# A fused attention and MLP kernel: batch 0 laid out in 96 partitions, a new placing of the second block, a bank read moved by one unit, and the last stores on three queues

## The chip, the cores and the metric

The kernel runs on one core of one Trainium2 chip. The metric is the device time of one execution in microseconds (us). Times below are medians of several executions, unless a single profiled execution is named. The profiled span of an execution is about 1.8 us shorter than its time.

## The reference

```python
# q, k, v: (8 batches, 8 heads, 576 positions, 64) f32;  w_in: 512 x 2048;  w_out: 2048 x 512
kv  = einsum('bhsd,bhse->bhde', k, v)
o   = einsum('bhsd,bhde->bhse', q, kv)
x   = o / sqrt(mean(o * o, axis=-1) + 1e-6) * g_norm        # -> 4608 tokens x 512
h   = x @ w_in
g   = maximum(h, 0) + alpha * minimum(h, 0)                 # alpha: one per column of h
out = g @ w_out                                             # 4608 x 512 f32
```

The 4608 tokens are cut into nine blocks of 512. A block's `h` is made in 16 units (`h_ps`, one for each 128 columns of d_ff, four matmuls of 512 columns). From block 1 on, the second product uses a scheme with seven half-size products instead of eight; they share three PSUM banks, called X, Y and Z. While block w makes its `h`, the tensor engine (PE) also does the seven products of block w-1 and the attention steps of block w+1: `t` (transpose q), `kv`, `ot` (the attention output), `ssq` (sum of squares, then `rstd` on ScalarE and the normalised `xt` on VectorE). Heads are worked on in pairs. A regroup is a copy that reorders a landed load for PE.

## The kernel before

Only the parts that the change and the argument touch; `# ...` marks cuts.

```python
# the start: two pairs of q and of k of batch 0 by the two hardware queues, the rest by GpSimd (queue q0)
def early_half(eng, nm, tag):
    st32[nm] = w_p.tile([P, H // 2, TPP * D], FP32, name=f"{nm}32", tag=tag)
    eng.dma_start(out=st32[nm][:],
        in_=srcs[nm][0, 0 : H // 2, 0:MAIN, :].rearrange("h (p t) d -> p h (t d)", t=TPP))
early_half(nc.sync, "q", "wsum2")
early_half(nc.scalar, "k", "wsum4")
# ...
for nm in ("q", "k", "v"):
    load_rem(0, nm)                      # the last 64 of 576 rows: 4 x 128 + 64
load_main(0, "v", 0, HH)
load_main(0, "q", HH, H)
load_main(0, "k", HH, H)
load_main(0, "v", HH, H)
for i in range(len(IN_CUTS) - 1):
    load_w_in(i)
# ... batch 1 and w_out in turn, then load_batch(2)
def keep_warm(n):                        # matmuls whose result nobody reads
    ps = ps_s.tile([P, W], FP32, name="warm_ps", tag="s")
    for i in range(n):
        nc.tensor.matmul(out=ps[:], lhsT=mask16[:], rhs=warm16[:], start=True, stop=True)
keep_warm(10)                            # and three more a little later
# ...
# block 1 (w == 1): where the attention steps of block 2 stand, by unit
for what, ats in (("kv", (1, 2, 3, 4)), ("t", (5, 6, 7, 9)),
                  ("ot", (7, 8, 10, 11)), ("ssq", (9, 10, 12, 13))):
# ...
# the products of the block before, 7 per unit in this order, and when a bank is read
Y_ORDER = (1, 6, 2, 7, 5, 4, 3)          # 1, 2 -> X;  6, 7, 4 -> Y;  5, 3 -> Z
Y_READS = {2: ("p1",), 5: ("u2",), 7: ("c11",), 9: ("u3",), 12: ("c22",), 14: ("c21",)}
# c22 reads Z after product 5; product 3 overwrites Z from unit 13 on
# ...
store_engines[0] = (nc.sync, nc.scalar)  # stores of the last block
```

## Time and profile before

| | before |
|---|---|
| time, median (range) | 298.06 us (297.89 to 298.69, 3 runs) |
| span of the profiled execution | 295.8 us |
| PE busy | 280.1 us, 95% |
| VectorE / ScalarE / GpSimd busy | 75% / 60% / 16% |
| first `h` matmul of block 0 / of block 1 | 17.93 / 49.17 us |
| end of PE's last matmul to end of the span | 4.93 us |

A line of the timeline gives start, length, engine, source line, operation, output and inputs, count, and in brackets PE's idle time just before with what ended it. Eleven matmuls of 512 columns in a row start 0.2155 us apart, and 16 of 256 columns 0.109 apart. But one matmul of 512 columns alone is shown 0.38 long. So the next one may start 0.165 before the shown end.

### The profile page before, as it was taken

To read this page: it belongs to the slowest core of one execution; us is meant where nothing else is said; L and a number is where in the kernel's file an instruction comes from. 1 tells how busy PE (TensorE), PEld (TensorE's weight loads), DVE (VectorE), ACT (ScalarE), POOL (GpSimd) and SP (SyncE) were. 2 spreads that over 40 slices of the span, in tenths; PEclk is the share of its full clock that TensorE was granted. 3 is DMA by queue.
4 is the path that set the end of the run, shared out by engine and by line. 5 is a ranking of instruction groups with operands and counts; after the bars stand their busy time and mean duration, and the time that the engine had idled before them with its cause. 6 is when DMAs were issued, how large, how long until landed. Compare 5 with 4: busy or idle time off the path is not lost.

```text
span 295.8 us, 5159 instructions
## 1 busy us (share of the span) xinstructions
PE 280.1 (95%) x1970; PEld 179.3 (61%) x1970; DVE 221.5 (75%) x419; ACT 176.1 (60%) x307; POOL 45.9 (16%) x64
## 2 busy tenths in 40 slices
PE   6779999998999999999999999999999999999993
PEld 2434454444666677666666677666666666666782
DVE  6559829679587877797778777877887788787861
ACT  3347367499758856775677668765745565433210
POOL 8644344440203120122002000000000000000000
PEclk9999999999999999999999999999999999999999
DMA  7999999999631990199019401110103011201223
GB/s 159 188 205 198 197 201 193 231 208 192 70 38 39 181 159 5 38 160 161 28 38 136 121 2 35 39 54 21 35 8 100 1 38 35 70 3 37 73 78 100
DMA packets 53081, 28.66 MB, mean 97 GB/s; under 512 B 15152, under 2 KB 52544, under 8 KB 53056
## 3 DMA queue, kind: packets, MB, share of 16 engines
q0 software_dynamic: 41376, 17.83, 48.5%
q1 hardware_dynamic: 10368, 9.32, 10.7%
q10 hardware_dynamic: 1312, 1.18, 1.4%
q8 instruction: 15, 0.25, 0.4%
q14 instruction: 10, 0.08, 0.1%
HBM read 36.71 MB, written 9.44 MB: 156 GB/s over the span
## 4 chain that ended last, share of the span: by engine, by line
PE 69%; DMA 18%; ACT 5%; issue 3%; DVE 2%; POOL 1%; DVEq 0%; POOLq 0%; ACTq 0%
PE h_ps L320 31%; PE yY L468 12%; PE yZ L468 10%; PE yX L468 9%; DMA qst<-in_q_dram 6%; DMA vst<-in_v_dram 5%; DMA w_in_sb<-in_moe_w_in_dram 5%; DMA ksb<-in_k_dram 2%; ACT m_sb L327 2%; PE qt_ps L238 2%; PE ssq_ps L294 2%; PE kv_ps L256 2%; PE ot_ps L278 2%; DVE y_sb L495 1%; ACT ksb L147 1%
## 5 line engine op out<-in xcount | busy, mean ns | idle before, releaser
L320 PE MATMUL h_ps<-xt,w_in_sb 128*128 128x512 f16 x576 | 145.3, 379 | 2.0 <-DVE gt L331 1.8
L331 DVE SCALAR_TENSOR_TENSOR gt<-m_sb,beta_sb,h_ps 128x512 f16<-128x512 f32 x144 | 106.9, 746 | 49.5 <-ACT m_sb L327 47.8
L327 ACT ACTIVATE m_sb<-h_ps 128x512 f32<-128x512 f32 x144 | 86.3, 600 | 65.0 <-PE h_ps L320 50.7
L320 PEld LDWEIGHTS <-w_in_sb 128*128 128x128 f16 x576 | 54.3, 98 | 48.3 <-issue 4.4
L468 PEld LDWEIGHTS <-s 128*128 128x128 f16 x512 | 50.1, 98 | 21.6 <-issue 2.5
L468 PEld LDWEIGHTS <-gt 128*128 128x128 f16 x384 | 37.6, 98 | 14.8
L468 PE MATMUL yY<-wsum,s 128*128 128x256 f16 x256 | 36.3, 273 | 0.0
L468 PE MATMUL yX<-w_out_sb,gt 128*128 128x256 f16 x256 | 35.1, 273 | 0.0
L284 ACT ACTIVATE sq_sb<-ot_ps 128x512 f16<-128x512 f32 x36 | 21.5, 605 | 17.5 <-PE ot_ps L278 17.5
L296 ACT ACTIVATE rstd<-ssq_ps,eps_t 128x512 f32<-128x512 f32 x36 | 24.7, 693 | 9.5 <-PE ssq_ps L294 9.5
L304 DVE SCALAR_TENSOR_TENSOR xt<-ot_ps,g2col,rstd 128x512 f16<-128x512 f32 x36 | 26.5, 745 | 4.2 <-ACT rstd L296 4.2
L250 ACT COPY qt_sb<-qt_ps 128x576 f16<-128x576 f16 x28 | 17.6, 641 | 6.0 <-PE qt_ps L238 6.0
L468 PE MATMUL yZ<-w_out_sb,s 128*128 128x256 f16 x128 | 17.5, 272 | 1.2 <-DVE y_sb L495 1.2
L468 PE MATMUL yY<-wsum,gt 128*128 128x256 f16 x128 | 17.6, 273 | 0.0
L468 PE MATMUL yZ<-wsum,s 128*128 128x256 f16 x128 | 17.6, 273 | 0.0
L345 PE MATMUL y<-w_out_sb,gt 128*128 128x512 f16 x64 | 17.1, 379 | 0.1
L132 POOL DMA_DIRECT2D vst<-in_v_dram x9 | 7.9, 876 | 59.3 <-PE kv_ps L256 52.7
L238 PE MATMUL qt_ps<-ident,qsb 128*128 128x128 f16 x160 | 14.1, 225 | 1.6 <-DVE qsb L520 0.9
L294 PE MATMUL ssq_ps<-sq_sb,mask 128*128 128x512 f16 x36 | 13.5, 379 | 1.4 <-ACT rstd L296 0.7
L278 PE MATMUL ot_ps<-qt_sb,kv_sb 128*128 128x512 f16 (+7 forms) x64 | 13.6, 286 | 0.9 <-DVE kv_sb L264 0.7
L256 PEld LDWEIGHTS <-ksb 128*128 128x128 f16 x160 | 11.6, 100 | 4.1 <-issue 1.3
L238 PEld LDWEIGHTS <-qsb 128*128 128x128 f16 x160 | 10.9, 100 | 5.2 <-DVE qsb L520 1.9
(57 smaller groups left out, 226.1 us busy)
## 6 DMA issues: line engine op xcount, KB each, us to landing
out_dram<-y_sb SPq DMA_DIRECT2D x72, 64.0 KB, 2.1
kst<-in_k_dram POOLq DMA_DIRECT2D x7, 512.0 KB, 12.4
qst<-in_q_dram POOLq DMA_DIRECT2D x7, 512.0 KB, 12.7
vst<-in_v_dram POOLq DMA_DIRECT2D x7, 512.0 KB, 12.7
out_dram<-y_sb SPq DMA_DIRECT2D x23, 128.0 KB, 2.0
w_out_sb<-in_moe_w_out_dram POOLq DMA_DIRECT2D x4, 512.0 KB, 16.5
w_in_sb<-in_moe_w_in_dram POOLq DMA_DIRECT2D x3, 512.0 KB, 12.6
out_dram<-y_sb SPq DMA_DIRECT2D x4, 256.0 KB, 6.9
```

The source lines that it names most:

```text
L238: nc.tensor.matmul(out=qt_ps[:, t * P : (t + 1) * P], lhsT=qs(t), rhs=ident16[:], is_transpose=True, start=(t == 0), stop=(t == NT - 1),)
L250: nc.scalar.copy(out=qts[b, j][:], in_=qt_ps[:, 0:S])
L256: nc.tensor.matmul(out=kv_ps[:], lhsT=ks(t), rhs=vs(t), start=(t == 0), stop=(t == NT - 1),)
L278: nc.tensor.matmul(out=ot_ps[:, n0 - w * W : n1 - w * W], lhsT=kvs[b, j][:], rhs=qts[b, j][:, n0 - b * S : n1 - b * S], start=True, stop=True,
L284: nc.scalar.activation(out=sq[:], in_=ot_ps[:], func=AF.Square)
L294: nc.tensor.matmul(out=ssq_ps[:], lhsT=mask16[:], rhs=sq[:], start=True, stop=True)
L296: nc.scalar.activation(out=rstd[:], in_=ssq_ps[:], func=AF.Abs_reciprocal_sqrt, bias=eps_t[:], scale=inv_d,)
L304: nc.vector.scalar_tensor_tensor(out=xts[w, j][:], in0=ot_ps[:], scalar=g2col[:], in1=rstd[:], op0=ALU.mult, op1=ALU.mult,)
L320: nc.tensor.matmul(out=h_ps[:], lhsT=w_in_blk(c, g), rhs=xts[w, c][:], start=(c == 0), stop=(c == NC - 1),)
L327: nc.scalar.activation(out=m_sb[:], in_=h_ps[:], func=AF.Relu, scale=-1.0)
L331: nc.vector.scalar_tensor_tensor(out=gts[w, i][:, r, :], in0=m_sb[:], scalar=beta_sb[:, g : g + 1], in1=h_ps[:], op0=ALU.mult, op1=ALU.add,)
L468: nc.tensor.matmul(out=bank, lhsT=lhs, rhs=rhs, start=fresh, stop=(c == NK - 1), skip_group_check=True,)
```

## The change

The intent has five parts, named as in the prediction. **A**: batch 0 is cut into 96 partitions of 6 positions, so no 64-row remainders are left; only one pair of q and of k goes by hardware queues, and fillers (matmuls that keep the clock up) stand between the small products of the start. Smaller moves belong to A too: the ten warm-up matmuls begin earlier, g_norm is loaded with alpha, and more banks take the first `h` groups. **B**: batch 2 is loaded as q, k, v, block 0's stores go by GpSimd's queue, and block 1's attention steps get other units and banks. **C**: copies and sums at the turn from block 1 to block 2 are spread. **D**: `c22` is read one unit earlier, in all blocks. **E**: `c21` of the last block is read one unit earlier and stored on three queues. Cut to its core:

```diff
+    T0 = next(n for n in range(NT, S) if S % n == 0)      # 6
+    P0 = S // T0                                          # 96
-    early_half(nc.sync, "q", "wsum2")
-    early_half(nc.scalar, "k", "wsum4")
+    early_pair(nc.sync, "q", "wsum2")
+    early_pair(nc.scalar, "k", "wsum4")
...
-    for nm in ("q", "k", "v"):
-        load_rem(0, nm)
-    load_main(0, "v", 0, HH)
-    load_main(0, "q", HH, H)
-    load_main(0, "k", HH, H)
-    load_main(0, "v", HH, H)
+    load0("v", 0, 2)
+    load0("q", 1)
+    load0("k", 1)
+    load0("q", 2, 2)
+    load0("k", 2, 2)
+    load0("v", 2)
+    load0("v", 3)
...
-    load_batch(2)
+    load_batch(2, ("q", "k", "v"))
-    store_engines = [(nc.sync,)]
+    store_engines = [(nc.gpsimd,)]
...
-    Y_READS = {2: ("p1",), 5: ("u2",), 7: ("c11",), 9: ("u3",), 12: ("c22",), 14: ("c21",)}
+    Y_READS = {2: ("p1",), 5: ("u2",), 7: ("c11",), 9: ("u3",), 11: ("c22",), 14: ("c21",)}
...
     step_t(0, 0, h_at(0))
+    keep_warm(2)
     step_kv(0, 0)
+    keep_warm(1)
     step_ot(0, 0)
+    # ... 13 fillers in all behind the first ten; three stood there before
...
-        ("kv", (1, 2, 3, 4)), ("t", (5, 6, 7, 9)), ("ot", (7, 8, 10, 11)), ("ssq", (9, 10, 12, 13))
+        ("t", (0, 2, 4, 5)), ("kv", (4, 5, 6, 7)), ("ot", (6, 8, 10, 12)), ("ssq", (9, 10, 12, 14))
-                        pool = O_POOL if what == "kv" and j % 2 else Q_POOL
+                        pool = Q_POOL if j % 2 == 0 else O_POOL if what == "kv" else S_POOL
...
+    REG_2 = {
+        0: (("k", 0),), 1: (("q", 1),), 2: (("k", 1),), 3: (("q", 2),), 4: (("k", 2),),
+        5: (("q", 3),), 6: (("k", 3),),
+    }
...
+    Y_READS[13] = Y_READS.pop(14)          # last block only
+            if what == "c21":
+                store_engines[0] = (nc.scalar, nc.gpsimd, nc.sync, nc.gpsimd)
```

More of the change, by code (lines that the diff above doesn't have):

```diff
@@ L44 @@
     NT = TPP + 1
+    T0 = next(n for n in range(NT, S) if S % n == 0)
+    P0 = S // T0
     NF = D_FF // P
     NC = D_MODEL // P
-    assert NC == NPAIR and 0 < REM < P
+    assert NC == NPAIR and 0 < REM < P and P0 <= P and H % 4 == 0
     inv_d = 1.0 / D
@@ L71, with early_pair @@
     st32 = {}
-    def early_half(eng, nm, tag):
-        st32[nm] = w_p.tile([P, H // 2, TPP * D], FP32, name=f"{nm}32", tag=tag)
+    def early_pair(eng, nm, tag):
+        st32[nm] = w_p.tile([P, 2, T0 * D], FP32, name=f"{nm}32", tag=tag)
         eng.dma_start(
-            out=st32[nm][:],
-            in_=srcs[nm][0, 0 : H // 2, 0:MAIN, :].rearrange("h (p t) d -> p h (t d)", t=TPP),
-        )
-    early_half(nc.sync, "q", "wsum2")
-    early_half(nc.scalar, "k", "wsum4")
+            out=st32[nm][0:P0],
+            in_=srcs[nm][0, 0:2, :, :].rearrange("h (p t) d -> p h (t d)", t=T0),
+        )
+    early_pair(nc.sync, "q", "wsum2")
+    early_pair(nc.scalar, "k", "wsum4")
     _set_id = list(get_activation_tables(nc.m.arch).keys()).index(
@@ L93 @@
     )
-    warm16 = const_p.tile([P, W], FP16, name="warm16")
-    nc.vector.memset(warm16[:], 0.5)
+    warm16 = ysb_p.tile([P, 2 * W], FP16, name="y_sb")[:, 0:W]
+    nc.vector.memset(warm16, 0.5)
     mask32 = const_p.tile([P, P], FP32, name="mask32")
@@ L105 @@
     nc.vector.memset(eps_t[:], 1e-6)
-    alpha_row = const_p.tile([NF, P], FP32, name="alpha_row")
-    nc.sync.dma_start(out=alpha_row[:], in_=moe_alpha[:].rearrange("(g p) -> g p", p=P))
-    g2col = const_p.tile([P, 1], FP32, name="g2col")
-    nc.sync.dma_start(out=g2col[0:64, :], in_=g_norm[:].unsqueeze(1))
-    nc.sync.dma_start(out=g2col[64:128, :], in_=g_norm[:].unsqueeze(1))
+    alpha_row = ysb_p.tile([P, D_MODEL], FP32, name="y_sb")
+    nc.sync.dma_start(out=alpha_row[0:NF, 0:P], in_=moe_alpha[:].rearrange("(g p) -> g p", p=P))
+    for r in range(P // D):
+        nc.sync.dma_start(
+            out=alpha_row[NF : NF + 1, r * D : (r + 1) * D], in_=g_norm[:].unsqueeze(0)
+        )
     NBUF = 3
+    HH = H // 2
     bufs = []
@@ L120, with load0, load_main @@
         for nm in ("k", "v", "q"):
-            n = 1 if nm == "v" else NT
+            n = 1 if nm == "v" else T0 if i == 0 else NT
             t[nm] = qkv_p.tile([P, n, H, D], FP16, name=f"{nm}sb{i}")
-            nc.vector.memset(t[nm][REM:P, n - 1, :, :], 0.0)
+            if i > 0 or nm == "v":
+                nc.vector.memset(t[nm][REM:P, n - 1, :, :], 0.0)
         bufs.append(t)
     stages = {}
-    def load_main(b, nm, h0, h1):
-        st = stages.get((b, nm))
-        if st is None:
-            st = stage_p.tile([P, H, TPP, D], FP16, name=f"{nm}st", tag=f"{nm}st")
-            stages[b, nm] = st
-        nc.gpsimd.dma_start(
-            out=st[:, h0:h1, :, :].rearrange("p h t d -> p h (t d)"),
-            in_=srcs[nm][b, h0:h1, 0:MAIN, :].rearrange("h (p t) d -> p h (t d)", t=TPP),
+    def load0(nm, j, n=1):
+        i, h = divmod(2 * j, HH)
+        if (0, nm, i) not in stages:
+            stages[0, nm, i] = stage_p.tile([P, HH, T0, D], FP16, name=f"{nm}st", tag=f"{nm}st")
+        nc.gpsimd.dma_start(
+            out=stages[0, nm, i][0:P0, h : h + 2 * n].rearrange("p h t d -> p h (t d)"),
+            in_=srcs[nm][0, 2 * j : 2 * (j + n), :, :].rearrange("h (p t) d -> p h (t d)", t=T0),
+        )
+    def load_main(b, nm):
+        st = stage_p.tile([P, H, TPP, D], FP16, name=f"{nm}st", tag=f"{nm}st")
+        stages[b, nm] = st
+        nc.gpsimd.dma_start(
+            out=st[:].rearrange("p h t d -> p h (t d)"),
+            in_=srcs[nm][b, :, 0:MAIN, :].rearrange("h (p t) d -> p h (t d)", t=TPP),
         )
@@ L153, in load_batch, with regroup0 @@
             load_rem(b, nm)
-            load_main(b, nm, 0, H)
+            load_main(b, nm)
+    def regroup0(nm, j, n=1):
+        i, h = divmod(2 * j, HH)
+        nc.vector.tensor_copy(
+            out=bufs[0][nm][0:P0, :, 2 * j : 2 * (j + n), :].rearrange("p t h d -> p h t d"),
+            in_=stages[0, nm, i][0:P0, h : h + 2 * n],
+        )
     def regroup_pair(b, nm, j):
@@ L190, in w_out_blk @@
         return w_out_sb[i][:, r, :]
-    HH = H // 2
-    for nm in ("q", "k", "v"):
-        load_rem(0, nm)
-    load_main(0, "v", 0, HH)
-    load_main(0, "q", HH, H)
+    load0("v", 0, 2)
+    load0("q", 1)
+    load0("k", 1)
     ident = const_p.tile([P, P], FP32, name="ident")
     make_identity(nc, ident[:])
-    load_main(0, "k", HH, H)
-    load_main(0, "v", HH, H)
+    load0("q", 2, 2)
+    load0("k", 2, 2)
+    load0("v", 2)
+    load0("v", 3)
     for i in range(len(IN_CUTS) - 1):
@@ L209, with keep_warm @@
     load_w_out(3)
-    load_batch(2)
-    def keep_warm(n):
-        ps = ps_s.tile([P, W], FP32, name="warm_ps", tag="s")
+    load_batch(2, ("q", "k", "v"))
+    warm_ps = ps_q.tile([P, W], FP32, name="warm_ps", tag="q")
+    def keep_warm(n, ps=warm_ps):
         for i in range(n):
-            nc.tensor.matmul(out=ps[:], lhsT=mask16[:], rhs=warm16[:], start=True, stop=True)
+            nc.tensor.matmul(out=ps[:], lhsT=warm16[:, 0:P], rhs=warm16, start=True, stop=True)
     keep_warm(10)
@@ L223, with rows, n_runs @@
     qts, kvs, xts = {}, {}, {}
+    def rows(b):
+        return P0 if b == 0 else P
+    def n_runs(b):
+        return T0 if b == 0 else NT
     def pair_cols(b, nm, j):
         def f(t):
+            n = rows(b)
+            if nm == "v" and b == 0:
+                h = 2 * j % HH
+                return stages[b, nm, 2 * j // HH][0:n, h : h + 2, t, :]
             if nm == "v" and t < TPP:
@@ L229, in f @@
             if nm == "v":
-                return bufs[b % NBUF][nm][:, 0, 2 * j : 2 * j + 2, :]
-            return bufs[b % NBUF][nm][:, t, 2 * j : 2 * j + 2, :]
+                return bufs[b % NBUF][nm][0:n, 0, 2 * j : 2 * j + 2, :]
+            return bufs[b % NBUF][nm][0:n, t, 2 * j : 2 * j + 2, :]
         return f
@@ L235, in step_t @@
         qs = pair_cols(b, "q", j)
-        qt_ps = pool[0].tile([P, NT * P], FP16, name="qt_ps", tag=pool[1])
-        for t in range(NT):
+        qt_ps = pool[0].tile([P, n_runs(b) * rows(b)], FP16, name="qt_ps", tag=pool[1])
+        c = 0
+        for t in range(n_runs(b)):
+            n = rows(b)
             nc.tensor.matmul(
-                out=qt_ps[:, t * P : (t + 1) * P],
+                out=qt_ps[:, c : c + n],
                 lhsT=qs(t),
-                rhs=ident16[:],
+                rhs=ident16[0:n, 0:n],
                 is_transpose=True,
                 start=(t == 0),
-                stop=(t == NT - 1),
+                stop=(t == n_runs(b) - 1),
             )
+            c += n
         qts[b, j] = attn_p.tile([P, S], FP16, name="qt_sb", tag=f"qt{j}")
-        if b == 0:
+        if b == 0 and j < 2:
             nc.vector.tensor_copy(out=qts[b, j][:], in_=qt_ps[:, 0:S])
@@ L254, in step_kv @@
         kv_ps = pool[0].tile([P, P], FP32, name="kv_ps", tag=pool[1])
-        for t in range(NT):
+        for t in range(n_runs(b)):
             nc.tensor.matmul(
@@ L260, in step_kv @@
                 start=(t == 0),
-                stop=(t == NT - 1),
+                stop=(t == n_runs(b) - 1),
             )
@@ L356, in store_rows @@
             b, r = divmod(n0 + i, S)
-            if r < MAIN:
-                t, p = divmod(r, P)
-                cnt = min(P - i, P - p)
-                rows = out[b * S : b * S + MAIN, :].rearrange("(p t) m -> t p m", t=TPP)
-                dst = rows[t, p : p + cnt, c0:c1]
+            np_, nt = (P0, T0) if b == 0 else (P, TPP)
+            if r < np_ * nt:
+                t, p = divmod(r, np_)
+                cnt = min(P - i, np_ - p)
+                grid = out[b * S : b * S + np_ * nt, :].rearrange("(p t) m -> t p m", t=nt)
+                dst = grid[t, p : p + cnt, c0:c1]
             else:
@@ L517, with cast0 @@
     Q_POOL, S_POOL, O_POOL = (ps_q, "q"), (ps_s, "s"), (ps_o, "o")
-    def cast_pair(nm, st, j, eng_copy):
+    def cast0(nm, eng_copy):
         eng_copy(
-            out=bufs[0][nm][:, 0:TPP, 2 * j : 2 * j + 2, :].rearrange("p t h d -> p h t d"),
-            in_=st[:, 2 * j : 2 * j + 2, :].rearrange("p h (t d) -> p h t d", t=TPP),
-        )
-    cast_pair("q", st32["q"], 0, nc.vector.tensor_copy)
-    cast_pair("k", st32["k"], 0, nc.scalar.copy)
-    step_t(0, 0, H_POOL)
-    cast_pair("q", st32["q"], 1, nc.vector.tensor_copy)
@@ L529, with h_at @@
-    cast_pair("k", st32["k"], 1, nc.scalar.copy)
-    step_t(0, 1, H_POOL)
-    keep_warm(3)
+            out=bufs[0][nm][0:P0, :, 0:2, :].rearrange("p t h d -> p h t d"),
+            in_=st32[nm][0:P0].rearrange("p h (t d) -> p h t d", t=T0),
+        )
+    def h_at(i):
+        return (ps_h, f"h{i}")
+    cast0("q", nc.vector.tensor_copy)
+    cast0("k", nc.scalar.copy)
+    step_t(0, 0, h_at(0))
+    keep_warm(2)
     step_kv(0, 0)
-    step_kv(0, 1, H_POOL)
+    keep_warm(1)
     step_ot(0, 0)
-    step_ot(0, 1)
@@ L536 @@
-    regroup(0, "q", HH, H)
-    step_t(0, 2, H_POOL)
-    step_t(0, 3, H_POOL)
-    regroup(0, "k", HH, H)
-    ssq_mm(0, 0, Q_POOL)
-    ssq_mm(0, 1)
-    norm(0, 0)
-    norm(0, 1)
-    alpha_ps = ps_h.tile([P, NF], FP32, name="alpha_ps", tag="h0")
+    regroup0("q", 1)
+    keep_warm(1)
+    step_t(0, 1, h_at(1))
+    regroup0("k", 1)
+    ssq_mm(0, 0)
+    keep_warm(1)
+    step_kv(0, 1, h_at(2))
+    keep_warm(1)
+    step_ot(0, 1)
+    alpha_ps = ps_y.tile([P, NF + 1], FP32, name="alpha_ps", tag="y")
@@ L545 @@
     nc.tensor.matmul(
-        out=alpha_ps[:], lhsT=alpha_row[:], rhs=ident[0:NF, 0:NF], is_transpose=True,
-        start=True, stop=True,
-    )
+        out=alpha_ps[:], lhsT=alpha_row[0 : NF + 1, 0:P], rhs=ident[0 : NF + 1, 0 : NF + 1],
+        is_transpose=True, start=True, stop=True,
+    )
+    regroup0("q", 2, 2)
+    keep_warm(1)
+    step_t(0, 2, h_at(0))
+    step_t(0, 3, h_at(1))
+    g2col = const_p.tile([P, 1], FP32, name="g2col")
+    nc.vector.tensor_copy(out=g2col[:], in_=alpha_ps[:, NF : NF + 1])
@@ L549 @@
     beta_sb = const_p.tile([P, NF], FP32, name="beta_sb")
     nc.vector.tensor_scalar(
-        out=beta_sb[:], in0=alpha_ps[:], scalar1=-1.0, scalar2=1.0, op0=ALU.mult, op1=ALU.add,
+        out=beta_sb[:], in0=alpha_ps[:, 0:NF], scalar1=-1.0, scalar2=1.0, op0=ALU.mult, op1=ALU.add,
     )
-    step_kv(0, 2)
-    step_kv(0, 3, Q_POOL)
-    step_ot(0, 2)
-    step_ot(0, 3, (ps_y, "y"))
+    norm(0, 0)
+    ssq_mm(0, 1, h_at(2))
+    keep_warm(2)
+    regroup0("k", 2, 2)
+    step_kv(0, 2, h_at(0))
@@ L557 @@
+    keep_warm(1)
+    step_kv(0, 3, h_at(1))
+    norm(0, 1)
+    step_ot(0, 2, (ps_y, "y"))
+    warm_late = ps_h.tile([P, W], FP32, name="warm_late", tag="h0")
+    keep_warm(1, warm_late)
+    step_ot(0, 3, Q_POOL)
+    keep_warm(1, warm_late)
     ssq_mm(0, 2)
-    ssq_mm(0, 3, Q_POOL)
+    keep_warm(1, warm_late)
+    ssq_mm(0, 3, h_at(2))
     norm(0, 2)
     norm(0, 3)
-    first = [h_bank() for g in range(3)]
-    m1_mm(first[0], 0, 0, (0, 1))
-    m1_mm(first[1], 0, 1, (0, 1))
-    m1_mm(first[0], 0, 0, (2,))
@@ L565 @@
-    m1_mm(first[1], 0, 1, (2,))
+    first = [ps_h.tile([P, W], FP32, name="h_ps", tag=f"h{g}") for g in range(3)]
+    for c in range(3):
+        for g in range(2):
+            m1_mm(first[g], 0, g, (c,))
     m1_mm(first[2], 0, 2, (0, 1, 2))
@@ L569 @@
         m1_evac(first[g], 0, g)
+    h_turn[0] = 2
     for g in range(3, NF):
-        m1_group(0, g, {3: Q_POOL, 4: S_POOL}.get(g))
+        m1_group(0, g, {3: S_POOL, 4: O_POOL, 5: O_POOL, 6: Q_POOL}.get(g))
         if g == 14:
             regroup(1, "k", 0, H)
+            for nm in ("k", "q"):
+                nc.vector.memset(bufs[0][nm][REM:P, TPP, :, :], 0.0)
     ys = {}
@@ L623 @@
     norm(1, 3)
-    regroup(2, "k", 0, H)
+    regroup(2, "q", 0, H)
     w_sum(4, 1)
@@ L633 @@
     y_out(ys[1], 0, 1)
+    store_engines[0] = (nc.sync,)
     h_turn[0] = 0
@@ L665, in attention @@
                     if w == 2 and what in ("kv", "ssq"):
-                        pool = O_POOL if what == "kv" and j % 2 else Q_POOL
+                        pool = Q_POOL if j % 2 == 0 else O_POOL if what == "kv" else S_POOL
                         (step_kv if what == "kv" else step_ssq)(w, j, pool)
-                    elif w == 2 and what == "ot" and j == 2:
-                        step_ot(w, j, (ps_y, "y"))
                     else:
                         ATT[what](w, j)
-    REG_1 = {12 + j: (("q", j),) for j in range(NPAIR)}
     REG_AT = {8 + 2 * j + i: ((nm, j),) for j in range(NPAIR) for i, nm in ((0, "q"), (1, "k"))}
+    Y3_AT = [(8, 8), (8, 8), (8, 8), (8, 9), (9, 9), (9, 10), (10, 10), (10, 10), (10, 11), (11, 11), (11, 12), (12, 12), (12, 13), (13, 14), (14, 15), (15, 16)]
+    REG_2 = {
+        0: (("k", 0),), 1: (("q", 1),), 2: (("k", 1),), 3: (("q", 2),), 4: (("k", 2),),
+        5: (("q", 3),), 6: (("k", 3),),
+    }
     for w in range(1, NW):
@@ L682 @@
                 unit_sums(w, u)
-            if w == 1 and u == 4:
-                regroup(2, "q", 0, H)
+            if w == 1 and u == 2:
+                regroup(2, "k", 0, H)
+            if w == 1 and u == NF - 1:
+                regroup(3, "q", 0, 2)
             if w == 2 and u == 0:
@@ L689 @@
             if w == 1:
-                if u < NF // 2:
-                    y_mm(ys[3], 0, 3, NF // 2 + u)
-                    if u == NF // 2 - 1:
+                for i in range(*Y3_AT[u]):
+                    y_mm(ys[3], 0, 3, i)
+                    if i == NF - 1:
                         y_out(ys[3], 0, 3)
@@ L700 @@
             if w == 1:
-                for k in {7: (0,), 9: (1,), 13: (2,)}.get(u, ()):
+                for k in {5: (0,), 8: (1,)}.get(u, ()):
                     s_sum(1, 1, k)
@@ L704 @@
             if w + 2 < B:
-                for nm, j in (REG_1 if w == 1 else REG_AT).get(u, ()):
+                for nm, j in REG_AT.get(u, ()) if w > 1 else ():
                     regroup_pair(w + 2, nm, j)
-            if w == 2 and u < 2:
-                for j in (2 * u, 2 * u + 1):
-                    regroup_pair(3, "k", j)
+            if w == 2:
+                for nm, j in REG_2.get(u, ()):
+                    regroup_pair(3, nm, j)
+                if u < 2:
+                    s_sum(1, u + 1, 2)
     w = NW - 1
     store_engines[0] = (nc.sync, nc.scalar)
+    Y_READS[13] = Y_READS.pop(14)
     for u in range(NF):
@@ L720 @@
         for what in Y_READS.get(u, ()):
+            if what == "c21":
+                store_engines[0] = (nc.scalar, nc.gpsimd, nc.sync, nc.gpsimd)
+                store_turn[0] = -1
             y_read(w, what)
+            store_engines[0] = (nc.sync, nc.scalar)
     y_read(w, "c12", (1,))
```

## The prediction

> **What bounds the kernel now.** I read the page's shares first, then the busy time in stretches, then the waits of the tensor engine (PE), and only then the DMA queues and the tail.
>
> ```profile
> PE 280.1 (95%) x1970; PEld 179.3 (61%) x1970; DVE 221.5 (75%) x419; ACT 176.1 (60%) x307; POOL 45.9 (16%) x64
> ...
> PE   6779999998999999999999999999999999999993
> ...
> DMA  7999999999631990199019401110103011201223
> ```
>
> PE is the bound, with 15.7 us not busy in 295.8. The slices show where: the first three, and the last. The DMA row is full for ten slices, the first 74 us, and then nearly free. So there are two regimes: a loading phase, in which the order and speed of the loads can hold PE, and a long steady phase that is PE alone. The waits of PE, all of them over 0.4 us except the warm-up's:
>
> ```profile
> PE h_ps L320 <- DVE gt L331: 1.8, 2, 1.5
> PE yZ L468 <- DVE y_sb L495: 1.2, 5, 0.2
> PE kv_ps L256 <- ACT rstd L296: 1.0, 1, 1.0
> PE qt_ps L238 <- DVE qsb L520: 0.9, 1, 0.9
> PE ssq_ps L294 <- ACT rstd L296: 0.7, 2, 0.6
> PE qt_ps L238 <- DVE qsb L149: 0.7, 1, 0.7
> ```
>
> The third and fourth lie in the first 20 us. The others are what PE loses later: 0.70 us at 57.6 (batch 2's q, just landed and regrouped), 0.56 and 0.19 at 65.1 and 68.7 (two uses of one bank), 1.50 at 74.2 (an evacuation behind a burst of regroup copies on ScalarE), and five times 0.24 us for the Z bank. With 0.32 at 25.7 and 0.14 after it that is 4.7 us after 20 us; nothing else is idle until the last matmul at 290.9.
>
> Now the loads. Queue q0 (GpSimd's) in two half microseconds, 5.0 to 5.5 and 8.5 to 9.0 (packets, MB, share of 16 engines):
>
> ```profile
> q0 software_dynamic: 253, 0.03, 100.8%
> ...
> q0 software_dynamic: 199, 0.10, 145.4%
> ```
>
> The first GpSimd load is issued at 1.25 us, but its first packet comes at about 5.05. Until 8 us the queue carries the three 64-row remainders in small pieces at 0.03 MB per half microsecond or less, then runs at 0.10. From there it is one train: each 512 KB lands 2.5 to 2.6 us after the one before. What the train means for PE is seen at w_out's third quarter, issued at 25.8, and its first use:
>
> ```profile
> DMA to landing us min/median/max: 16.6/16.6/16.6
> ...
> 42.26 0.59 PE L345 MATMUL y<-w_out_sb,gt 128*128 128x512 f16 x2
> ```
>
> It lands at 42.4; the second matmul of the pair, the first to need it, starts at 42.47. Batch 1's v lands at 39.8 and is used at 40.05. PE does not wait there, but has no slack: **a faster prologue is worth only what the train itself comes earlier.**
>
> **What the Trainium skill says.** "DMA: Bandwidth & Descriptors", Specifications, puts the smallest transfer for line rate at 512 B and says that the engine does read-modify-write below it. The remainders, of 128 B each when written, agree: 0.03 MB against 0.10. The same page, section "Issuing engines are not separate DMA queues", says that transfers of all three issuers share the same 16 engines and interleave. The trace agrees: from 53 to 54 us, beside block 0's stores (q1, 77.4%), q0 falls to 0.05 MB per us from about 0.20, and q's last 512 KB of batch 2 takes 5.4 us instead of 2.6. Its section "Anatomy of one DMA — SWDGE (gpsimd) path" gives 2.0 us plus bytes/436e3 for a GpSimd transfer. With 1 MB read, that is 4.4 us; this trace has 5.8 to 6.0 for such a load when the queue is otherwise empty, so I count longer. "TensorE: Matmul & The Clock Gate", Part 1, has a cold PE at half rate until one busy window of about 3.4 us. The first ten matmuls of 512 columns take 4.45 us, 0.43 each, twice the 0.216 of later; the clock column reads 1.00 there and does not show it.
>
> **Part by part.**
>
> *A, the start.* Removed: three remainder loads with their DVE memset and the 4-byte pieces of g_norm. The two hardware loads carry one pair of 0.29 MB each instead of two pairs of 0.52. Moved to q0: 5 x 0.295 = 1.475 MB of fp16, where it was 1.245 with the remainders. Before, the last piece of batch 0 lands at 14.42. After: first packet at 4.4 to 5.05 (the hardware loads end about a microsecond sooner, but whether they held the queue back isn't shown), 0.4 for the ramp, 1.475 / 0.2 = 7.4, and 1.0 to landing: 13.2 to 13.85. The train gains 0.6 to 1.2 us; I take **0.9**. The computing chain alone gains more: k of pairs 2 and 3 at about 12, two regroups of 0.6, products, square, rsqrt, norm at the durations of the old chain (0.3, 0.6, 0.7, 0.75) put the last norm at about 17.7 instead of 19.77. This 2.1 us, and the 0.32 at 25.7 that the extra banks save, turns into waits at 35 to 42 us for the difference. The 13 fillers lie in idle time of PE and cost nothing; a warm PE shortens some of the chain, which isn't the bound either.
>
> *B, block 1.* Batch 2's order becomes q, k, v; block 0's stores follow in the same queue, so nothing cuts in. Without stores v would land at 54.1 - 0.9 = 53.2. Block 1 starts at 49.17 - 0.9 = 48.3; four groups (0.86), two transposes (0.28), one y matmul (0.22) and the fifth group with its transpose later the first kv product comes at 53.7. Slack: 0.5 us. So the 0.70 goes, and alternating the ssq banks takes away 0.56 and 0.19. As DVE gets some 18.8 us of work in these 19.5 us, I give back 0.3: **1.15**.
>
> *C, the turn to block 2.* The burst of ScalarE copies is spread over seven units. But the y bank of block 0 is now read only at block 1's end: the copy (0.58) stands behind one evacuation (0.60), so X's first product waits about 0.4; and unit 1 takes the bank that unit 0 just filled, 0.2 + 0.6 + 0.75 against 1.04 of other PE work: 0.4 or so stays. 1.50 - 0.75 = **0.75**.
>
> *D, the bank read.* The Z bank's third reader starts at product 96, in unit 13; its data are read on DVE after unit 11 instead of 12. One unit is about 1.9 us, the wait 0.24: it goes, five times: **1.2**.
>
> *E, the tail.* Before, DVE's last addition ends at 291.42, but the last store goes out at 292.65 behind three others on its queue and lands 2.3 later; the span ends 0.85 after that. Now the c21 addition runs at 289.2, its four stores go to three queues, and the last halves find both hardware queues free: issued at 291.45, landed at 293.6. The second GpSimd store is issued at about 290.8 and needs 2.6 to 3.5 (1.6 to the first packet of a quiet queue): 293.4 to 294.3. Against 294.95: 0.65 to 1.3, taken as **1.1**.
>
> Sum: 0.9 + 1.15 + 0.75 + 1.2 + 1.1 = 5.1 us. 298.06 - 5.1 = **293.0 us**, 1.7% faster.
>
> **The rivals.** (1) *The train decides everything to 42 us and does not move*: GpSimd's queue has a fixed start-up, ramps slowly, and the extra 0.23 MB eats what the remainders gave. For it: 3.8 us from first issue to first packet, against 1.6 on a quiet queue. Then A is 0 to 0.2 and the time 293.8. (2) *GpSimd starts as soon as the hardware loads thin out.* q0's first packet comes just when q1 thins (5.0 us). Then A is 1.5 to 1.9 and the time about 292.1. Against it: at 53 us q0 keeps a third of the engines beside q1, so mere sharing wouldn't have kept it at zero. (3) *New waits*: v of batch 2 is late for unit 4, or block 0's six stores hold GpSimd's sequencer (0.5 to 0.9 us each, from 47 to 52) so long that batch 3's q is late for the DVE regroup at block 1's end. I have it landing near 64, needed at 67. If one of them happens, 1 to 2 us come back: 294 to 295. (4) *GpSimd's last stores end last* with the 5 us and more that its loads need in a busy queue: the tail gains nothing or loses 0.5, time 294.1 to 294.6.
>
> **Range and chances.** D and the removal of the ScalarE burst are the surest, 2 us. A spreads by 0.7 each way, B and C together by 0.7, E by 0.7, and they are nearly independent: about 1.3 us, so 291.3 to 294.8 for eight in ten. The 2% line is 292.1, 0.9 below my number: 0.30 for faster. Slower by 2% would need an outright stall of 11 us: 0.02.
>
> **What would show it.** Right: w_out's third quarter lands 0.6 to 1.2 us earlier, PE now waits for DMA at 35 to 42 us by about 1.5 in sum, and has no wait over 0.3 us on batch 2's q, none on the Z bank, and under 1 us at the turn to block 2; the last store lands within 3.0 us of the last matmul. A is wrong if that quarter moves less than 0.4 or more than 1.5; B if PE waits for v or k of batch 2; E if a GpSimd store is the last to land. The whole is wrong if PE's idle time after 45 us isn't cut by about 3 us.

## The result, and the profile after

| | before | after |
|---|---|---|
| time, median (range) | 298.08 us (297.89 to 298.69, 4 runs) | 291.36 us (290.8 to 292.0, 4 runs) |
| ratio, 95% interval | | 0.9772 (0.9746 to 0.9797) |
| span of the profiled execution | 295.8 us | 290.2 us |
| PE busy | 280.1 us, 95% | 280.6 us, 97% |

A ratio is the mean time of one kernel's runs over that of the other's runs of the same rounds, so it is not quite the ratio of the medians quoted. The change gains 6.7 us, or 2.3%. Foretold were 5.1 us and 1.7%: the time lies at the low edge of the range, and on the other side of the 2% line than the likeliest case. A repeat (`after_again`, below) had 291.45 us and a span of 289.3; its first profile, the one of this section, is of the slowest of four executions (292.0), and below it is said where that shows.

The page after, as the first lines of the prediction show it for before:

```profile
PE 280.6 (97%) x1988; PEld 179.5 (62%) x1988; DVE 221.2 (76%) x420; ACT 177.2 (61%) x307; POOL 50.1 (17%) x72
...
PE   7899999989999999999999999999999999999994
...
DMA  7999999999709990199019401110112011201223
```

PE has the same work (18 matmuls more) in 5.6 us less; the second and third slices went from 7 and 7 to 8 and 9. The DMA row is full for ten slices as before. The waits of PE after (two of 0.2 us before 11 us are left out):

```profile
PE warm_ps L235 <- DVE y_sb L99: 1.5, 1, 1.5
PE kv_ps L288 <- DMA vst<-in_v_dram: 0.8, 2, 0.5
PE ot_ps L310 <- DVE xt L336: 0.8, 1, 0.8
PE ot_ps L310 <- DVE kv_sb L296: 0.6, 3, 0.3
PE kv_ps L288 <- ACT qt_sb L282: 0.3, 1, 0.3
PE y L377 <- DMA w_out_sb<-in_moe_w_out_dram: 0.3, 1, 0.3
PE h_ps L352 <- DVE gt L363: 0.3, 1, 0.3
```

All six waits that the prediction listed are gone or small: `h_ps` for `gt` went from 1.8 to 0.3, the five waits of `yZ` and the waits for `rstd` and batch 2's q aren't there. New are a wait of `ot_ps` for `xt` (0.84 at 62.8) and one for `kv_sb` (0.31 at 59.4), both in block 1, and two for loads at 35.7 and 38.9 (0.32 and 0.36), which the repeat's list doesn't have.

**The Z bank.** PE's timeline where a product first overwrites Z, before:

```profile
98.06 0.71 PE L468 MATMUL yY<-wsum,gt 128*128 128x256 f16 x5
99.02 0.38 PE L468 MATMUL yZ<-w_out_sb,s 128*128 128x256 f16 x2 [0.24 <-DVE y_sb L495]
```

and the same place after:

```profile
95.59 0.71 PE L501 MATMUL yY<-wsum,gt 128*128 128x256 f16 x5
96.14 0.38 PE L501 MATMUL yZ<-w_out_sb,s 128*128 128x256 f16 x2
```

After, the Z product starts 0.55 us after the five Y products began, 5 x 0.109. Before, it starts 0.96 after. The wait cost **0.41 us**, though the bracket says 0.24: the rest lies under the shown length of the last Y matmul, which reaches beyond the time when the next could have begun. "TensorE: Matmul & The Clock Gate" of the Trainium skill, section "Single matmul latency", gives a warm matmul a constant part of 166 ns beside its columns; this trace agrees, with 0.38 shown against 0.2155 from start to start. A wait of less than that shows no idle time at all:

```profile
219.72 0.71 PE L468 MATMUL yY<-wsum,gt 128*128 128x256 f16 x5
220.45 0.38 PE L468 MATMUL yZ<-w_out_sb,s 128*128 128x256 f16 x2
```

This is one block of before where the list of waits names nothing; it lost 0.73 - 0.55 = 0.18 us. So seven blocks lost time here, not five: five times 0.4 and twice 0.18.

**The queue of loads.** In the half microsecond from 4.0 to 4.5 (packets, MB, share of 16 engines), before:

```profile
q1 hardware_dynamic: 93, 0.10, 55.7%
q10 hardware_dynamic: 93, 0.10, 54.4%
```

and after:

```profile
q0 software_dynamic: 58, 0.04, 76.7%
q10 hardware_dynamic: 42, 0.05, 36.9%
q1 hardware_dynamic: 33, 0.01, 12.7%
```

GpSimd's queue has its first packet at 3.99 instead of 5.08 (3.71 to 3.81 in the nine other profiles of this start): the hardware loads were cut by almost half, and q0 begins when their bulk is through. Landings from here on are read from the packed trace. w_out's third quarter lands at 41.32 in this profile and at 40.32 to 40.94 in the nine others; with the old start it was 42.39, 41.99 and 41.91. By the medians the train of loads is 1.3 us earlier. In the first profile the last piece of w_in took 3.34 us (21.12 to 24.46) where the nine others had 2.61 to 3.10. With it w_out's third quarter came 0.84 later than in the repeat, block 1 began 0.84 later, and the span is 0.9 longer. What held that piece up isn't known.

**The tail.** The last group of PE and the last issues of the sync queue, before:

```profile
288.99 1.91 PE L468 MATMUL yZ<-w_out_sb,s 128*128 128x256 f16 x16
...
290.51 2.39 SPq L367 DMA_DIRECT2D out_dram<-y_sb  x4
```

and after, with GpSimd's:

```profile
284.16 1.91 PE L501 MATMUL yZ<-w_out_sb,s 128*128 128x256 f16 x16
...
285.08 2.00 SPq L400 DMA_DIRECT2D out_dram<-y_sb  x3
...
285.36 1.10 POOL L400 DMA_DIRECT2D out_dram<-y_sb  x2 [131.43 <-DVE y_sb L526]
```

From PE's last end to the end of the span it was 4.93 us and is 4.13. VectorE's last addition ends at 286.58 and its stores go out at 286.6, where before they stood 1.2 us in line. The GpSimd stores land at 287.64 and 288.34, and the last packet of GpSimd's queue ends at 287.94. The sync and scalar queues end theirs at 288.39 and 288.56: a hardware queue is last.

**Where the 6.5 us lie.** Times of PE's timeline, before against the repeat of after, from start to start, so that hidden waits are counted (block 1 ends where its last `h` matmul lets the first X product start; the Z row is taken out of the row of the turn):

| stretch | before | after (repeat) | gain | predicted |
|---|---|---|---|---|
| A: to the first `h` matmul of block 1 | 49.17 | 47.22 | 1.95 | 0.9 |
| B: block 1 | 22.33 | 21.90 | 0.43 | 1.15 |
| C: the turn and block 2 without Z | 31.67 | 30.73 | 0.94 | 0.75 |
| D: Z bank, seven blocks | | | 2.34 | 1.2 |
| E: PE's end to span's end | 4.93 | 4.12 | 0.81 | 1.1 |
| sum | | | 6.47 | 5.1 |

D is 1.94, the difference of the stretches 103.57 to 278.50 (before) and 99.85 to 272.84 (repeat), from the second to the eighth time that X is begun, and 0.40 for the block ahead of them, which lasts 32.07 us before and 31.67 with D alone. The spans differ by 295.82 - 289.35 = 6.47.

### The profile page after: what moved, and what is told of

It is laid out like the page before. It is cut to its first block, busy times and chain, and to the rows that moved or that the text cites. A ratio compares the mean times of both kernels' runs of the same rounds, so it can differ in the third digit from the quotient of the medians.

```text
span 290.2 us, 5214 instructions
## 1 busy us (share of the span) xinstructions
PE 280.6 (97%) x1988; PEld 179.5 (62%) x1988; DVE 221.2 (76%) x420; ACT 177.2 (61%) x307; POOL 50.1 (17%) x72
## 4 chain that ended last, share of the span: by engine, by line
PE 83%; DMA 12%; DVE 1%; issue 1%; ACT 1%; POOL 1%; DVEq 0%; POOLq 0%
PE h_ps L352 38%; PE yY L501 14%; PE yZ L501 10%; PE yX L501 9%; DMA vst<-in_v_dram 5%; DMA w_in_sb<-in_moe_w_in_dram 5%; PE kv_ps L288 3%; PE ot_ps L310 3%; DMA qst<-in_q_dram 2%; PE ssq_ps L326 2%; PE qt_ps L269 2%; PE y L377 2%; DVE gt L363 1%; ACT m_sb L359 1%; DVE xt L336 0%
## 5 line engine op out<-in xcount | busy, mean ns | idle before, releaser
L316 ACT ACTIVATE sq_sb<-ot_ps 128x512 f16<-128x512 f32 x36 | 21.3, 597 | 17.3 <-PE ot_ps L310 16.8
L400 POOL DMA_DIRECT2D out_dram<-y_sb x8 | 4.4, 550 | 139.1 <-DVE y_sb L526 131.4
L282 ACT COPY qt_sb<-qt_ps 128x576 f16<-128x576 f16 x30 | 18.7, 637 | 5.8 <-PE qt_ps L269 5.7
L143 POOL DMA_DIRECT2D vst<-in_v_dram x7 | 6.2, 888 | 48.4 <-PE kv_ps L288 44.8
L288 PEld LDWEIGHTS <-ksb 128*128 128x128 f16 (+1 forms) x164 | 11.4, 98 | 4.5 <-DVE ksb L169 1.5
L288 PE MATMUL kv_ps<-vst,ksb 128*128 128x128 f16 (+1 forms) x136 | 12.6, 219 | 1.4 <-DMA vst<-in_v_dram 0.8
L453 DVE TENSOR_TENSOR s<-s,gt 128x512 f16<-128x512 f16 x32 | 13.5, 421 | 0.5
```

What stands on the lines that cost most here:

```text
L282: nc.scalar.copy(out=qts[b, j][:], in_=qt_ps[:, 0:S])
L288: nc.tensor.matmul(out=kv_ps[:], lhsT=ks(t), rhs=vs(t), start=(t == 0), stop=(t == n_runs(b) - 1),)
L316: nc.scalar.activation(out=sq[:], in_=ot_ps[:], func=AF.Square)
L453: nc.vector.tensor_sub(out=t[:], in0=sums[w, 1, k][:], in1=a11)
```

## The experiments

All thirteen runs gave results within the reference's tolerance. "Before" had medians of 297.8 to 298.1. Edits are against the kernel named.

### The whole change again: after_again

No edit.

> The changed kernel once more, as it is. The profiled execution of its first look was the slowest of four (292.0 beside 290.8 to 291.6), so 290.8 to 292.0 again, median near 291.3, if that spread belongs to the kernel. If the first look was a bad draw, all within 0.5 us.

Measured: 291.45 us (291.12 to 291.52, 4 runs), ratio 0.978 (0.9765 to 0.9795). The gain stands against its own runs of the kernel before (297.98).

### D alone, and all but D: bank_only and bank_back

```diff
# bank_only: the kernel before with
-    Y_READS = {... 12: ("c22",), 14: ("c21",)}
+    Y_READS = {... 11: ("c22",), 14: ("c21",)}
# bank_back: the changed kernel with that line as before
```

> The kernel before with one number changed: the second bank read after unit 11 instead of 12. By the prediction's step D (five visible idle pieces of 0.24 us) it gains 1.2 us: 296.9. By the block lengths (from one block's first X product to the next's: 0.41, 0.40, 0.18, 0.17, 0.38 shorter, and one more of 0.41 inside block 2) it gains 2.3 us: 295.8, and the blocks that showed no idle get 0.17 shorter too.

> The changed kernel with the second bank read back after unit 12. Step D as predicted: 1.2 us slower than the changed kernel. Block-length reading: 2.3 us slower, with waits of Z for the DVE of 0.24 us visible and 0.41 from start to start.

Measured: bank_only 295.85 us, ratio 0.9928 (0.9913 to 0.9944): 2.1 us less. bank_back 294.06, ratio 0.9873 (0.9855 to 0.9891): 2.6 us more than the changed kernel. In both, the times from first X product to first X product tell it: a steady block takes 30.42 us with the late read and 30.01 with the early one. With the wait back, its line is there again, and the same 0.96 from start to start:

```profile
94.94 0.71 PE L501 MATMUL yY<-wsum,gt 128*128 128x256 f16 x5
95.90 0.38 PE L501 MATMUL yZ<-w_out_sb,s 128*128 128x256 f16 x2 [0.25 <-DVE y_sb L528]
```

So D is worth 2.1 to 2.6 us, about twice the 1.2 that the idle column adds up to.

### Block 1 and the turn as before: block1_back

```diff
# the changed kernel with these back as before
-    load_batch(2, ("q", "k", "v"))
+    load_batch(2)
-    store_engines = [(nc.gpsimd,)]
+    store_engines = [(nc.sync,)]
# and the units and banks of block 1, the regroups and the sums of the turn
```

> The changed kernel with block 1 and its turn to block 2 as before (order k, v, q of batch 2, stores of block 0 by sync, old places of attention, y and regroup steps). The prediction gave these 1.15 + 0.75 = 1.9 us. The two traces say 0.41 for block 1 and 0.95 for the turn, so 1.4 us slower than the changed kernel; the waits for batch 2's q (0.70), for ssq (0.56, 0.19) and of h at block 2 (1.5) come back, those of ot (0.84, 0.31) go.

Measured: 292.72 us (292.57 to 293.42), ratio 0.983 (0.9813 to 0.9847): B and C are worth 1.27 us together, not 1.9. From block 1's first `h` matmul to where X could start it takes 22.12 us, against 21.90 with the new placing: B itself is worth 0.2 us here. The old waits are back (0.50 for q, 0.55 and 0.19 for the ssq bank, and 1.50 at the turn), but two new ones are gone, and they were nearly as long. PE's timeline of the changed kernel (first profile) for these:

```profile
59.40 0.38 PE L310 MATMUL ot_ps<-qt_sb,kv_sb 128*128 128x128 f16 x2 [0.31 <-DVE kv_sb L296]
...
62.78 0.39 PE L310 MATMUL ot_ps<-qt_sb,kv_sb 128*128 128x128 f16 x2 [0.84 <-DVE xt L336]
```

There are two `ot` banks. The second `ot` (59.40) gets the one that the fourth `kv` held, which VectorE has only just evacuated. The third (62.78) gets that of the first `ot`, which is free only when `ssq`, `rstd` and `xt` have gone through three engines.

### A better block 1: block1_better

```diff
# the changed kernel with
-    ("ssq", (9, 10, 12, 14))
+    ("ssq", (8, 10, 12, 14))
-    pool = Q_POOL if j % 2 == 0 else O_POOL if what == "kv" else S_POOL
+    pool = Q_POOL if j % 2 == 0 else O_POOL if what == "kv" and j == 1 else S_POOL
             if w == 2 and u == 0:
                 h_tags[0] = ("h1", "h2")
+                h_turn[0] = 1
```

> The changed kernel with three small moves against the waits that it brought into block 1 and its turn: the first ssq of batch 2 one unit earlier (the third ot product waited 0.84 us for its norm), the fourth kv product in another bank (the second ot product waited 0.31), and the two banks of block 2 taken in turn (0.31). With 0.16 us of each that the idle column doesn't show, up to 1.9 us faster, 289.5; by the idle columns alone 1.4, 290.0.

Measured: **289.92 us** (289.59 to 290.55), ratio 0.9736 (0.9715 to 0.9756), the fastest of all: 1.5 us less than the changed kernel. Between 12 us and the end, PE's list of waits is empty. Block 1 to the first X product takes 21.11 us instead of 22.15, and the next block 30.16 instead of 30.48. So the new waits were real costs, and B as placed gave back most of what it had won.

### The start alone: start_only

```diff
# the changed kernel with B, C, D and E as before
```

> Batch 0's new start alone: the changed kernel with block 1, the bank read and the last stores as before. The prediction's part A gave 0.9 us (0.6 to 1.2). The second look at the changed kernel has w_out's third quarter at 40.5 us instead of 42.4 and no wait of the tensor engine for a load, so the start should be worth 1.8 to 2.1 us: near 296.1.

Measured: 296.12 us (295.42 to 296.38), 1.7 us less than before (297.82), ratio 0.9934 (0.9914 to 0.9955). A is worth 1.7 us, its smaller moves included, which no run separates. w_out's third quarter lands at 40.94, and the first matmul that needs it was due at 40.89: PE is as fast as the train here.

### What sets the first packet of GpSimd's queue: rems_late and two_pairs_hw

```diff
# rems_late: the kernel before with the three remainder loads behind the other loads of batch 0
-    for nm in ("q", "k", "v"):
-        load_rem(0, nm)
...
     load_main(0, "v", HH, H)
+    for nm in ("q", "k", "v"):
+        load_rem(0, nm)
# two_pairs_hw: the changed kernel with two pairs of q and k by the hardware queues
+    early_pair(nc.sync, "q", "wsum1", 1)
+    early_pair(nc.scalar, "k", "wsum3", 1)
-    load0("q", 1)
-    load0("k", 1)
# ... and pair 1 is then copied from these tiles
```

> The kernel before with the three remainder loads of batch 0 moved behind its other GpSimd loads (slower in the start, since the transposes wait for them). Asked only when q0's first packet comes. If the remainders are what held the queue back, at 4.0 us as in the changed kernel; if the hardware loads or a fixed start-up hold it, at 5.0 as before.

> The changed kernel with two pairs of q and k by the hardware queues again (four loads of 0.29 MB), and two GpSimd loads fewer. If the hardware loads keep q0 waiting, its first packet moves from 3.9 to some 5.2 us and v of pair 0 lands at 8.5 instead of 7.3; the total of bytes is the same and the train comes at the same time or up to 0.5 us later, the time within 1 us of the changed kernel's. If q0 has a start-up of its own, its first packet stays at 3.9 and the train comes 1 us earlier.

rems_late was looked at once (304.01 us, state unknown, PE waits 7.4 us for a remainder); only its queue is used. It still has no packet of q0 before 5.0. So the remainders, slow as they are, didn't hold the queue back. The same half microsecond as above, 4.0 to 4.5, in two_pairs_hw:

```profile
q1 hardware_dynamic: 74, 0.11, 82.2%
q10 hardware_dynamic: 33, 0.04, 28.1%
```

and 6.0 to 6.5, where q0 at last runs (six packets came in the half microsecond before):

```profile
q0 software_dynamic: 74, 0.06, 75.5%
q10 hardware_dynamic: 44, 0.05, 40.0%
q1 hardware_dynamic: 18, 0.00, 5.7%
```

With more bytes by hardware, q0 starts two microseconds later than in the changed kernel (5.94 against 3.99). The first packet follows the bytes of the hardware loads: 0.59 MB, 3.7 to 4.0 us; 1.05 MB, 5.0 to 5.1; 1.19 MB, 5.94. It is these loads that hold it back, not a start-up of its own. The time was 292.51 us (291.78 to 292.61), ratio 0.981 (0.9789 to 0.983), 1.1 more: PE waits 1.99 us for v at 8.59, and block 0's first `h` matmul starts at 17.31 instead of 15.99. w_out's third quarter lands at 40.73, no later than elsewhere, so here it is the chain of computing that costs, not the train.

### The stores of block 0: stores0_sync

```diff
# the changed kernel with
-    store_engines = [(nc.gpsimd,)]
+    store_engines = [(nc.sync,)]
```

> The changed kernel with block 0's stores on sync, from where they cut into batch 2's loads. Three stores of 256 KB took 2.8 us from the loads in the kernel before, and v of batch 2 now is the last and has less than half a microsecond of slack in the first trace: it lands up to 2.8 us later, and the first kv product of batch 2 waits for it: 1.5 to 2.5 us slower. If the loads have more slack than I think, no change.

Measured: 293.61 us (293.1 to 295.63), ratio 0.9866 (0.9841 to 0.989), 2.2 us more. PE's timeline:

```profile
54.49 0.38 PE L288 MATMUL kv_ps<-vst,ksb 128*128 128x128 f16 x4 [1.91 <-DMA vst<-in_v_dram]
```

With the stores in another queue they cut into the loads of batch 2; v lands at 54.45 and block 1 waits. In the first profile of the changed kernel v landed at 53.27 and was used at 53.43. So the stores in GpSimd's queue are what makes B's order of loads work at all, with 0.2 us to spare.

### The fillers: no_fillers and fillers_only

```diff
# no_fillers: the changed kernel without the 13 keep_warm behind the first ten
# fillers_only: the kernel before with 15 fillers of 512 columns between the small products, where 3 stood
```

> The changed kernel without the fillers behind the first ten. By the prediction they cost and gain nothing: within 0.3 us. If a cold tensor engine stretches the start, the last norm comes up to 1 us later, and the time with it by as much, as the second look showed no wait for loads at 35 to 42 us.

> The kernel before with one thing added: fifteen more matmuls of 512 columns between the small products of the start (three became four, and 2, 1, 4, 2 and 2 were put in elsewhere), on a bank that is free there. Loads, regroups and everything from 20 us on stay as they were. Theory 1 (the train of loads bounds the first 42 us of the kernel before, as the prediction had it, and the tensor engine's clock does not): the small products and the first h group run at the warm rate, but what they gain turns into waits for w_out's third quarter, which still lands at 42.4: 0 to 0.3 us faster than before, so 297.7 to 298. Theory 2 (the computing chain bounds the start in both kernels, and the warm engine is worth by itself what it is worth in the changed kernel, 1.5 us): 1.0 to 1.6 us faster, 296.4 to 297, with no wait for a load of w_out. Theory 3 (the fillers sit in the way of the small products that release the next steps, 0.1 to 0.2 us each): 0 to 1 us slower.

no_fillers: 292.91 us (292.58 to 294.05), ratio 0.9834 (0.9816 to 0.9852), 1.5 us more. PE's busy time in stretches, with the granted clock (the share of full speed that PE is given) ahead of the last two columns (DMA share and GB/s), of the changed kernel:

```profile
6.00:12.00 6.00, 4.80 (x43) 2.52 (x41) 3.13 (x10) 2.01 (x4) 4.52 (x6) 1.00 1.26 185
12.00:18.00 6.00, 5.51 (x39) 2.48 (x37) 3.93 (x7) 4.10 (x7) 3.91 (x5) 1.00 1.34 202
```

and of no_fillers:

```profile
6.00:12.00 6.00, 3.93 (x27) 2.22 (x27) 2.74 (x8) 1.92 (x3) 4.36 (x6) 0.63 1.31 196
12.00:18.00 6.00, 5.48 (x32) 2.86 (x32) 3.07 (x8) 3.89 (x7) 3.91 (x5) 0.50 1.33 202
```

Without fillers the clock is at half from 7.61 to 21.27 us (clock records of the packed trace), though after the warm-up PE's longest idle gap is 1.31 us (ahead of 6.43). All five executions have a mean clock of 0.974 to 0.982, the four of the repeat 0.997 to 1.0. The profile is of the slowest of the five (294.05), so its 2.9 us of span over the repeat is more than the typical loss. In it the first `h` matmul starts at 17.96, as late as before the change (17.93), and PE never waits for the train: it uses batch 1's v at 41.01, which landed at 38.38.

fillers_only: 297.46 us (297.4 to 297.83) against 298.08, ratio 0.9978 (0.9963 to 0.9993): 0.6 us less, with an interval from 0.2 to 1.1. (There are twelve fillers more than before, not fifteen, as the expectation says.) Block 0's `h` matmuls start 0.70 earlier (17.23 instead of 17.93), but the first X product only 0.19 earlier (71.31 instead of 71.50). On the way, w_out's third quarter (landed at 41.91) holds up the pair at 41.58, shown 0.75 long instead of 0.59, and batch 2's q now costs 1.04 where it was 0.70:

```profile
57.44 0.45 PE L239 MATMUL qt_ps<-ident,qsb 128*128 128x128 f16 x5 [1.04 <-DVE qsb L149]
```

In this profile an earlier start turns into waits for the train, as theory 1 has it. But the 0.70 isn't the fillers' alone. By the clock records PE had full clock from 7.18 here and only from 11.50 in the profile of before, where three fillers at 8.61 take 1.49 us, against 1.03 for four at 8.40 here. bank_only, with no more fillers than before, had it from 7.81, and its `h` began at 17.26; there too the gain was lost at batch 2's q (1.17 us), and X began at 71.52. What the fillers change by time may be how often the clock fails. Of 44 executions of before, 17 have a mean clock under 0.9925 and take 298.3 us in the mean; 20 with 0.997 or more take 297.8. The six of fillers_only all have 0.995 or more. The timed gain lies between the two theories' figures, and what it consists of isn't settled.

### The tail: tail_back and tail_two_queues

```diff
# tail_back: the changed kernel with the last stores as before
# tail_two_queues: the early read of c21 stays, its stores go to two queues
-                store_engines[0] = (nc.scalar, nc.gpsimd, nc.sync, nc.gpsimd)
+                store_engines[0] = (nc.scalar, nc.sync)
```

> The changed kernel with its last stores as before: c21 read after unit 14 and two queues. The prediction's part E gave 1.1 us; from the last matmul to the span's end it is 4.13 us in the changed kernel's first trace and 4.9 in the kernel before, so 0.8. Slower by 0.8 to 1.1 us.

> The changed kernel with c21 read after unit 13, as changed, but all last stores on the two hardware queues. If the earlier read is what gains, within 0.3 us of the changed kernel; if the third queue is, slower by 0.8.

tail_back: 292.29 us (291.63 to 292.56), ratio 0.9805 (0.9788 to 0.9822), 0.8 more. tail_two_queues: 291.54 (291.2 to 292.71), ratio 0.9795 (0.9775 to 0.9814). From PE's last end to the span's end it is 4.92 us with tail_back, 4.30 with two queues and 4.12 in the repeat. So E is worth 0.8: about 0.6 by the early read, and 0.2 by the third queue, which the times alone don't resolve (0.1).

## Why the prediction missed

**D is the term that was mis-sized most, and the step that failed.** "One unit is about 1.9 us, the wait 0.24: it goes, five times: 1.2". The mechanism was right: the read one unit earlier takes the wait away in every block. The size was read from the idle column. From start to start each wait cost 0.41, and two blocks lost 0.18 that the list of waits doesn't show at all. It measured 2.1 (alone) and 2.6 (taken out), 2.34 in the profiles.

**A: the rule held, its numbers did not.** The prediction said that a faster start is worth only what the train comes earlier. With fillers that is so: PE reaches w_out's third quarter and batch 1's v as they land (in the repeat v landed at 37.96, and its first product started at 38.01, 0.31 later than the matmuls before it allowed). The sign named for this, waits for DMA "at 35 to 42 us by about 1.5 in sum", came as 1.1 us in the first profile and 0.4 in the repeat, from start to start. What failed is "first packet at 4.4 to 5.05": it came at 3.7 to 4.0. Rival 2 named the mechanism, that GpSimd's queue starts as the hardware loads thin out, and its 1.5 to 1.9 us; it was set aside because at 53 us q0 had kept a third of the engines beside q1. two_pairs_hw and rems_late show that this doesn't carry over to the start. The last piece of batch 0 landed 1.04 us earlier, at 13.35, inside the window foretold; the train 1.3 by the medians, the start 1.7 by time.

**A, second step: the fillers.** That they "cost nothing" was right; that a warm PE shortens a chain "which isn't the bound either" was wrong for this kernel. Without them the clock halves, the chain of computing is the bound again, and 1.5 of the 1.7 us are gone. The last norm ended at 17.91 and 17.76 (repeat), near the 17.7 foretold; in no_fillers it ended at 19.77, the same as before. By these times the two parts need each other: fillers alone give 0.6, and an earlier train without fillers gives 1.7 - 1.5 = 0.2, by subtraction.

**B failed in its result.** "So the 0.70 goes, and alternating the ssq banks takes away 0.56 and 0.19" came true, and so did v with little slack (0.5 foretold, 0.2 seen). But the 0.3 given back for VectorE's load was too small, and the cause was another: the new placing asks for an `ot` bank while both are held, and waits of 0.31 and 0.84 came. Of 1.15 stayed 0.43 against before, and 0.2 against the old placing with the new start. Rival 3 had new waits, but looked for them at v and at batch 3's q, where there were none. block1_better shows the loss to be the placing's, by moving one step and two banks.

**C and E** were near: 0.94 against 0.75, and 0.81 against 1.1. At the turn 0.31 of the 1.50 stayed, plus 0.25 us by which the first X product is late. In the tail no GpSimd store was last, as E assumed and against rival 4.

**The sum.** D, A and C gave 1.14, 1.05 and 0.19 more than foretold, B and E 0.72 and 0.29 less; 5.1 became 6.5. As errors of both signs met, the time came out only just at the edge of the range. But the range treated the terms as spreading around their values, and D, which was called among the surest, was low by a fault of reading that repeats in every block. Smaller slips of reading, with no weight in the sum: the list of waits "over 0.4 us" leaves out two in the first 20 us (0.69 for `kv_sb` at 16.10, 0.53 for `sq_sb` at 17.23), and the last store of before lands at 294.78, 2.1 us after its issue and not 2.3.

## What to carry to other kernels

Read what a wait costs from the starts of the instructions around it, not from the idle time ahead of one: where a shown length reaches beyond the time at which the next instruction could start (by 0.165 us here), the shown idle time is too short by as much, and small waits in a repeated block vanish from the list altogether. When a stage has two bounds close together, here a train of loads and a chain of small products, moving one is worth little until the other moves too, so test each part by taking it out of the whole as well as by doing it alone. And when a wait for one bank is scheduled away, ask which bank the moved step will find taken.

## What the Trainium skill lacked or had wrong

- "TensorE: Matmul & The Clock Gate", "Why this matters for your kernels", asks for no idle gaps of PE over about 3 us to keep the clock. That wasn't enough here: in no_fillers it was at 0.50 from 7.6 to 21.3 us with no gap above 1.31 us after the warm-up. Another section of the page, on a second failure mode, does tell of short idles between groups, but gives no length or share for them. In the 3.41 us before the clock fell (4.20 to 7.61) PE is shown busy for 1.47 us. In bank_only, which has only three fillers behind the first ten, the clock held at 1.00 from 7.81 to 11.22 with 2.01 us busy. In the changed kernel the 13 fillers kept it at 1.00, worth 1.5 us.
- "Perfetto Trace Analysis", "Tensor Engine Instruction", says that a matmul's end is estimated, but not what follows for waits: the idle time shown between matmuls is too short by some 0.165 us each time (0.24 shown, 0.41 lost), and below that nothing is shown (0.18 lost).
- "DMA: Bandwidth & Descriptors", "Queues, rings and completion order", has the engines take turns between queues. At the start GpSimd's queue got no packet from 4.0 to 4.5 us beside two hardware loads of 0.52 MB, though its first load was issued at 1.25, and began when they thinned out (5.08; 3.7 to 4.0 with one load of 0.29 MB each; 5.94 with two such on each queue). Whether its descriptors were not yet ready or it was not served isn't shown.
